# Reordering the head of a sparse-attention and mixer kernel: queries on ScalarE's queue, keys in two halves, and a new hand order

## The chip, the cores and the metric

The kernel runs on one core of one Trainium2 chip. The core has TensorE (PE) for matmuls, which writes its products to eight PSUM banks; VectorE (DVE), ScalarE (ACT) and GpSimd (POOL) for the rest; and 16 DMA engines, fed from queues that SyncE (SP), ScalarE and GpSimd issue to. All times are device microseconds. A kernel's time is the median over its runs. Beside the timed runs there is one profiled execution; its span, from its first to its last recorded work, is what the views of the profile divide up.

## The reference

Two steps are chained. The first is attention with a block-sparse mask over batch 4, 8 heads, 768 positions and head dimension 64. Positions fall into 24 blocks of 32. A query block sees its neighbours, the first and the last block, and three sampled blocks; the first and last query blocks see all.

```python
scores = scale * np.matmul(q, k.transpose(0, 1, 3, 2))
...
scores = np.where(mask, scores, -1000000000.0)
scores = scores - np.max(scores, axis=-1, keepdims=True)
attn = np.exp(scores)
attn = attn / (np.sum(attn, axis=-1, keepdims=True) + 1e-09)
return np.matmul(attn, v).astype(np.float32)
```

The second is a mixer on the attention's result x (4 x 768 x 512): a low-rank mixing over positions, then a channel network of width 2048.

```python
xt = x.transpose(0, 2, 1)
h = xt @ U @ V
u = x + h.transpose(0, 2, 1)
ch = np.maximum(u @ w_ch1, 0.0) @ w_ch2
return (u + ch).astype(np.float32)
```

Inputs and output are 32-bit floats; the kernel multiplies in 16 bits.

## The kernel before

**Tiles.** The 8 heads of a batch make 4 pairs, so there are 16 pairs (`NPAIR`). Per head, the 768 keys are 6 chunks of 128. A score product (`score`, L690) puts one key chunk against all 768 queries: two matmuls of 384 columns (L697) into two PSUM banks, followed by one exponential on ScalarE (L706). `two_scores` (L711) does two chunks at once in three banks: four matmuls (L716), one exponential over 1536 columns (L724). The exponentials of a chunk are the weights of six small matmuls with the values (`value_product`, L400), which sum over the chunks and give the numerator and, through a column of ones in `vts`, the denominator.

**The mask.** For the four pairs of batch 0 the mask is part of the product: beneath the 64 rows of a head's queries in `qres` stand 24 rows with a one-hot of the query's block, and beneath its keys in `kres` 24 rows with the bias (0 or -240) of that block for every key. For later batches the mask is a 0/1 tile (`mask`), made during the first pairs by `mask_part` (L654) from a copy of the bias rows (`kmask`) and multiplied on VectorE after the exponential (L756).

**The head of the kernel** is written out in order (L239 to L326). The sampled blocks, the first head's queries, keys and a constant `small` are loaded. `small` holds three things: the fixed mask, the block numbers, and a 128 x 128 identity in 16 bits (`id16`). VectorE computes the bias from the sampled blocks (L289 to L296). Loads are cast to 16 bits (`first_cast`, L208), turned by matmuls against the identity (`first_turn`, L214; three per half of the positions), and evicted to `qres[0]` and `kres[0]` (`first_row`, L281). `mask_half` (L270) multiplies the bias with the one-hot, and `mask_row` (L278) evicts it to the mask rows of one head for half of the keys. `keep_warm` (L262) issues matmuls on constants whose result nobody reads. The second head of the pair is cast on GpSimd and turned later (`last_turn`, L334, the word `Z`). The second buffers `qres[1]` and `kres[1]` and `kmask` are filled by `second_set` (L191): one-hots from memory, mask rows copied from the first set by DMA.

**The order.** On TensorE, VectorE, ScalarE and SP the program order is the order of work (`manual_schedule`); on GpSimd the same sequence arises. After the head, the order is the string `PLAN` (L432 to L457), of one word per step. A capital letter issues TensorE work, with the PSUM bank as digit: S and B are one and two score chunks, A one chunk's value product, Z and R turn queries or keys, K makes a part of the mask, M, X, Y, D and E mix over positions, P, C and U are products with `w_ch1` (L587), W and L with `w_ch2` (L611, L636), Q and H are scores of later batches (L741), V the values of a whole head there. A small letter issues what the oldest product of its kind still lacks on another engine: e an exponential, t, z, y, v, k, d, m and g evictions or sums on VectorE, p the multiplication by the mask, a or b a relu on ScalarE or VectorE, f and l the final sum and its store.

A product may not be written to a bank before the reader of its earlier content is done. `psm` (L107) hands out banks 2, 5 and 7 in turn, `psc2` (L100) banks 3 and 0; the two mask products lie in banks 6 and 2, the turned queries in banks 4 and 0, the turned keys in 5 and 7.

**Loads.** `load_qk` (L143) and `load_v` (L156) load a pair and cast it on GpSimd; `loads(i)` (L763) issues those of pair i + 2, the first when pair 0 begins. `w_ch1` is loaded on GpSimd's queue behind pair 3's loads, `w_ch2` by `hold` (L775) when pair 4 begins.

Of the kernel before, what the change touches and what calls it, by code (L numbers as in the profile page):

```python
# [19 lines left out]
P = 128  # L20
# [3 lines left out]
def kernel(  # L24
# [43 lines left out]
    small_np = np.zeros((P, NB + 1 + P // 2), np.float32)  # L68
    small_np[:NB, :NB] = (ms_np - 1.0) * -MASK_BIAS
    small_np[:NB, NB] = ii  # L70
    small_np[:, NB + 1 :] = np.eye(P, dtype=np.float16).view(np.float32)

    small_dr = nc.inline_tensor(small_np, name="small_const")
    ohT_dr = nc.inline_tensor(ohT_np, name="one_hot_const")
# [36 lines left out]
    small = consts.tile([P, NB + 1 + P // 2], FP32)  # L111
    ms = small[0:NB, 0:NB]
    iota = small[0:NB, NB : NB + 1]
    id16 = small[:, NB + 1 :].bitcast(FP16)
# [54 lines left out]
    def first_load(h, n, queue):  # L169

        src, nm = ((q, "qld"), (k, "kld"))[n]
        if h == 0:
            lds[nm] = ldpool.tile([P, 2, T, D], FP32, tag="ld" + nm, name=nm)
            sts[0, nm] = stpool.tile([P, T, 2, D], FP16, tag="st" + nm, name="st" + nm)
        if h == 1:
            nc.gpsimd.memset(lds[nm][0:1, h, 0, 0:1], 0.0)
        queue.dma_start(
            out=lds[nm][:, h], in_=src[0, h].rearrange("(p t) d -> p t d", t=T)
        )

# [10 lines left out]
    def second_set():  # L191
        for h in range(2):
            one_hot(1, h)
# [14 lines left out]
    def first_cast(h, n, copy):  # L208
        nm = ("qld", "kld")[n]
        copy(out=sts[0, nm][:, :, h], in_=lds[nm][:, h])  # L210
# [3 lines left out]
    def first_turn(n, c):  # L214

        if n == 1:
            pt = psm([P, HS], FP32)
        elif c == 0:
            pt = pw[:, 1, 0:HS]
        else:  # L220
            pt = psc2()[:, 0, 0:HS]
        first_out[n, c] = pt
        for j in range(3):
            nc.tensor.matmul(  # L224
                pt[0:D, j * P : (j + 1) * P],
                sts[0, ("qld", "kld")[n]][:, 3 * c + j, 0],
                id16,
                start=(j == 0), stop=(j == 2), skip_group_check=True,
            )

    with tc.manual_schedule(
# [13 lines left out]
        first_load(0, 0, nc.sync)  # L245
        nc.scalar.dma_start(out=small, in_=small_dr.ap())
        first_load(0, 1, nc.scalar)
        for h in (1, 0):
            nc.vector.memset(qres[0][(slice(D, P), slice(0, D))[h], h, :], 0.0)
            one_hot(0, h)  # L250
        nc.vector.memset(bias, 0.0)
# [26 lines left out]
        def mask_row(h, c, copy):  # L278
            copy(out=kres[0][mrows[h], h, c * HS : (c + 1) * HS], in_=pks[c][mrows[h]])

        def first_row(n, c, copy):  # L281
            copy(
                out=(qres, kres)[n][0][drows[0], 0, c * HS : (c + 1) * HS],
                in_=first_out[n, c][0:D],
            )

        neq = consts.tile([P, NB, 3], FP32)
# [14 lines left out]
        for n in range(2):  # L302
            first_cast(0, n, nc.vector.tensor_copy)
        for c in range(2):
            first_turn(0, c)
            first_row(0, c, nc.scalar.copy)
        mask_half(0)
        mask_row(0, 0, nc.vector.tensor_copy)
        first_turn(1, 0)
        first_row(1, 0, nc.scalar.copy)  # L310
        first_turn(1, 1)
        mask_half(1)
        keep_warm(2, 256)
        first_row(1, 1, nc.vector.tensor_copy)
        mask_row(0, 1, nc.vector.tensor_copy)
        mask_row(1, 0, nc.vector.tensor_copy)
        mask_row(1, 1, nc.vector.tensor_copy)
# [3 lines left out]
        nc.vector.memset(Ut, 0.0)  # L321
        load_v(0)
        load_qk(1)
        second_set()
        load_v(1)
        load_mix()  # L326


# [105 lines left out]
    S0 S3 e e S5 B0 e Z7 e S3 z Z6 e z B0 A7 A e R6 S3 t A R5 e A B0 t A K6 e A S3 k v A5 A e K6  # L434
    k B0 A A e K7 A K6 k S3 k A K7 e v B0 k S3 e M6 e A5 A m R7 A t B0 K6 R3 e k A A t S6 A e v
    S0 D2 S3 e d A7 A e A S0 K6 A e S3 k K2 A e S5 k A e v S3 R2 e S5 t S0 e M7 e S3 m D2 e B5 d
    A0 D1 e A A d A S3 D2 A e d K1 S5 k R7 e S3 t A S1 e v A5 A e A S3 S6 e K2 A e A k A S3 v B0
    e K7 M6 e k S3 m X5 K7 e A6 Y k A B0 y X7 Y e S3 y E5 A e A g A R7 S0 t A e v S4 S2 e A7 A e
    R1 E6 A t A g A A Q v e e M6 X7 m Y P6 y p H U7 e p H b C e p H b U7 e p H b U6 e p E1 a g p
    V7 Q v e e V6 U7 v p U0 a P1 b C p P6 a C E7 Q a g U6 e e U7 b P6 b p U0 C a U7 p a Q b X6 Y  # L440
    e e P7 y C P6 b C p U0 b a p V7 Q v e e V6 W7 v p U0 W a p Q U6 e e W b U6 p W b p Q f W6 e
    e W p U2 U0 a p a V7 Q v W e e p V7 U2 v W a p Q f W7 e e W p U6 W a p Q U6 e e W b U6 p f a
    p V0 U1 v a V7 U6 v Q a M6 e e W7 m W p D6 U0 d U1 p a D2 D3 a U6 d d D0 U5 a d D6 U1 a d W
    a W Q f D6 W7 e e d W p D0 D6 W d d p W Q f W6 e e W p W W p Q f e e V7 U6 v p a V0 U2 v p
    U7 a U6 a Q b U7 e e U6 b U7 b p U2 a U6 p a U7 a Q b U6 e e U7 b U6 b p U2 a p a V7 Q v e e
    V6 U7 v p U0 b U1 a W6 p a Q W e e W p W U7 f p Q a U6 e e W7 b W p U1 p a V6 Q v W e e p V6
    U2 v W a p Q f W6 e e W p U7 W b p Q U7 e e W b U7 p f U2 a p a V0 v V7 W6 v Q M7 e e W m U7
    p D0 U1 a d U2 p a D7 D3 a U0 d d U1 a D5 D0 a U2 d d U7 a W a W Q f D7 W6 e e d W p D1 D7 W
# [452 lines left out]
```

## Time and profile before

| what | value |
|---|---|
| median of 7 runs | 284.09 us (283.49 to 286.18) |
| profiled execution | 284.99 us |
| its span | 283.1 us |
| PE busy, share of span | 275.5 us, 97% |
| DVE busy | 194.3 us, 69% |
| ACT busy | 178.2 us, 63% |
| POOL busy | 74.1 us, 26% |
| first score on PE | 8.13 us |
| first exponential on ACT | 9.01 us |
| first `Q` on PE | 45.04 us |
| end of the last matmul in the chain | 276.9 us |

A busy PE is one that has a matmul in flight; their ends are modelled and overlap, so 97% is not 97% of its peak. Between 13.5 and 45 us three engines are nearly full (PE 31.1 of 31.5 us, ACT 29.9, DVE 28.1); between 48 and 226 us PE alone is (178.0 of 178.0, ACT 126.8, DVE 140.8). The granted clock (PEclk) reads full speed in every slice. In the lists below a line of the chain gives start, length and what it was; a line of a timeline gives start, length, engine, source line, operation, output and input with their shapes, how many, and in brackets the idle time before and what ended it.

### The profile page before, as it was taken

Reading aid. Unit: us, or ns where it says so; the run is one execution under the profiler, and the core shown is the slowest. Engines: PE = TensorE matmul, PEld = TensorE weight load, DVE = VectorE, ACT = ScalarE, POOL = GpSimd, SP = SyncE. Lnnn points to the kernel's source line nnn. Section 1 sums busy time; section 2 is a strip of 40 time slices with the busy share of each in tenths; the row PEclk is TensorE's granted clock in tenths of the full one; section 3 lists DMA queues with packets and bytes.
Section 4 is the critical chain, followed back from the end, with each engine's and each line's share of the span. In section 5 each row is a group of like instructions: output and inputs, shape, how many; then the busy total and the mean of one; then the engine's idle time right before and its main releaser. Section 6 shows DMA issues by size and latency. Waiting matters only on the chain.

```text
span 283.1 us, 6704 instructions
## 1 busy us (share of the span) xinstructions
PE 275.5 (97%) x2768; PEld 160.9 (57%) x2768; DVE 194.3 (69%) x347; ACT 178.2 (63%) x206; POOL 74.1 (26%) x164
## 2 busy tenths in 40 slices
PE   7899999999999999999999999999999999999993
PEld 3577775656464654656465654656546645555552
DVE  4599988998867898878677888777577871003411
ACT  3799998897687647687868555697876303551100
POOL 5367204926536050073443050070000000000000
PEclk9999999999999999999999999999999999999999
DMA  6699997999672564556260744641010062002021
GB/s 169 196 287 300 196 197 179 251 205 242 206 220 80 131 188 130 138 144 204 67 197 37 218 131 102 179 120 23 27 47 31 15 132 88 0 0 76 0 93 57
DMA packets 49118, 37.53 MB, mean 133 GB/s; under 512 B 30464, under 2 KB 45600, under 8 KB 49088
## 3 DMA queue, kind: packets, MB, share of 16 engines
q1 hardware_dynamic: 45968, 32.61, 41.9%
q0 software_dynamic: 2688, 4.19, 8.8%
q8 instruction: 21, 0.34, 0.5%
q10 hardware_dynamic: 432, 0.31, 0.4%
q14 instruction: 9, 0.07, 0.1%
HBM read 27.67 MB, written 6.29 MB: 120 GB/s over the span
## 4 chain that ended last, share of the span: by engine, by line
PE 91%; DVE 3%; DMA 2%; ACT 2%; issue 0%; SPq 0%; DVEq 0%; ACTq 0%
PE ps L587 30%; PE ps L611 29%; PE ps L400 12%; PE ps L741 10%; PE ps L697 3%; PE ps L529 2%; PE ps L716 2%; DMA qld<-in_q_dram 1%; ACT est L724 1%; ACT est L706 1%; PE ps L656 1%; DMA out_dram<-of 1%; DVE qres L686 1%; PE ps L636 1%; PE ps L670 1%; PE ps L224 1%
## 5 line engine op out<-in xcount | busy, mean ns | idle before, releaser
L750 ACT ACTIVATE est<-ps 128x1536 f16<-128x1536 f32 x72 | 100.4, 1451 | 38.6 <-PE ps L741 38.6
L587 PE MATMUL ps<-uT,w1t 128*128 128x384 f16 x512 | 94.3, 326 | 0.0
L611 PE MATMUL ps<-w2t,tT 128*128 128x512 f16 x368 | 87.1, 379 | 0.0
L756 DVE TENSOR_TENSOR est<-est,mask 128x1536 f16<-128x1536 f16 x72 | 69.6, 972 | 15.1 <-ACT est L750 14.9
L599 ACT ACTIVATE tT<-ps 128x384 f16<-128x384 f32 x90 | 43.1, 496 | 43.4 <-PE ps L587 42.2
L587 PEld LDWEIGHTS <-w1t 128*128 128x128 f16 x512 | 47.6, 98 | 36.3 <-issue 5.8
L611 PEld LDWEIGHTS <-tT 128*128 128x128 f16 x368 | 34.4, 98 | 39.6 <-issue 3.8
L400 PEld LDWEIGHTS <-est 128*128 128x128 f16 x1152 | 40.8, 97 | 7.0 <-issue 1.9
L400 PE MATMUL ps<-vt,est 128*128 128x65 f16 x1152 | 43.4, 193 | 0.0
L140 POOL CAST stqld<-qld 128x192 f16<-128x192 f32 x40 | 15.3, 423 | 85.5 <-DMA qld<-in_q_dram 59.9
L619 DVE TENSOR_TENSOR of<-xf,ps 128x512 f32<-128x512 f32 x23 | 15.7, 684 | 27.8 <-PE ps L611 25.8
L601 DVE TENSOR_SCALAR tT<-ps 128x384 f16<-128x384 f32 x38 | 21.1, 556 | 18.7 <-PE ps L587 18.1
L741 PE MATMUL ps<-qpl,kpl 64*128 64x512 f16 (+1 forms) x288 | 31.3, 325 | 0.0
L706 ACT ACTIVATE est<-ps 128x768 f16<-128x768 f32 x30 | 22.5, 815 | 1.5 <-PE ps L697 1.5
L741 PEld LDWEIGHTS <-kpl 64*128 64x128 f16 x288 | 11.8, 94 | 15.9 <-issue 10.4
L140 POOL CAST stkld<-kld 128x192 f16<-128x192 f32 x40 | 19.5, 528 | 1.3 <-DMA kld<-in_k_dram 1.3
L477 DVE TENSOR_TENSOR xh<-ps,rcp 128x384 f16<-128x384 f32 x32 | 17.8, 558 | 1.1
L477 DVE TENSOR_TENSOR xf<-ps,rcp 128x384 f32<-128x384 f32 x32 | 17.5, 548 | 0.0
L541 DVE TENSOR_TENSOR xh<-xh,ps 128x384 f16<-128x384 f16 x28 | 15.4, 551 | 1.7 <-PE ps L529 1.6
L542 DVE TENSOR_TENSOR xf<-xf,ps 128x384 f32<-128x384 f32 x28 | 15.4, 550 | 0.0
L140 POOL CAST vt<-vld 128x192 f16<-128x192 f32 x40 | 15.1, 416 | 0.5 <-DMA vld<-in_v_dram 0.5
L697 PE MATMUL ps<-qres,kres 128*128 128x384 f16 x60 | 14.7, 343 | 0.3
(83 smaller groups left out, 151.8 us busy)
## 6 DMA issues: line engine op xcount, KB each, us to landing
vld<-in_v_dram SPq DMA_DIRECT2D x16, 384.0 KB, 4.7
out_dram<-of SPq DMA_DIRECT2D x23, 256.0 KB, 2.0
qld<-in_q_dram SPq DMA_DIRECT2D x15, 384.0 KB, 5.1
kld<-in_k_dram SPq DMA_DIRECT2D x15, 384.0 KB, 4.9
w1t<-in_moe_w_ch_dram POOLq DMA_DIRECT2D x4, 512.0 KB, 8.2
w2t<-in_moe_w_ch_dram POOLq DMA_DIRECT2D x4, 512.0 KB, 7.9
qld<-in_q_dram SPq DMA_DIRECT2D x2, 192.0 KB
uT<-xh SPq DMA_TRANSPOSE x14, 2.8
```

Of the source, the lines that this page charges most:

```text
L140: last = nc.gpsimd.tensor_copy(out=dst[:, h, ts], in_=ld[:, h, ts])
L400: nc.tensor.matmul(pav[:, sc, :], est[:, n, sc * P : (sc + 1) * P], vts[b % 2][:, 2 * hp + h, g, 0 : D + 1], start=(g == 0 and sc == 0), s ...
L477: nc.vector.tensor_tensor(out=dst, in0=pav[:, :, 0:D], in1=rcp[:, :, None].broadcast_to([P, T, D]), op=ALU.mult,)
L587: nc.tensor.matmul(pt, w1t[:, cc, jj * P : (jj + 1) * P], bts[b].uT[cc][:, c * HS : (c + 1) * HS], start=(cc == 0), stop=(cc == NCC - 1), ...
L599: nc.scalar.activation(out=dst, in_=pt, func=AF.Relu)
L601: nc.vector.tensor_scalar_max(out=dst, in0=pt, scalar1=0.0)
L611: nc.tensor.matmul(po, tts[b, c, jj][:, s * P : (s + 1) * P], w2t[:, jj, :], start=(jj == 0), stop=(jj == NJJ - 1),)
L697: nc.tensor.matmul(ps[:, c], kT[:, h, g * P : (g + 1) * P], qT[:, h, c * HS : (c + 1) * HS], start=True, stop=True,)
L706: lambda: nc.scalar.activation(out=dst, in_=ps, func=AF.Exp, scale=0.125),
L741: nc.tensor.matmul(units[h][:, u * S + lo : u * S + hi], kT[drows[h], g * P : (g + 1) * P], qT[drows[h], lo:hi], start=True, stop=True, sk ...
L750: nc.scalar.activation(out=both[h], in_=units[h].rearrange("p (g n) -> p g n", g=2), func=AF.Exp, scale=0.125,)
L756: lambda: nc.vector.tensor_mul(out=both[h], in0=both[h], in1=mask[:, 2 * j : 2 * j + 2, :]),
```

## The change

The identity gets a constant of its own (`eye_dr`), so `small` shrinks to 24 rows of 25 numbers. The first load on ScalarE's queue is now the first head's queries, and the identity follows; on SP's queue stand the sampled blocks, `small`, the first half of the first head's keys (three of the six position groups), the two one-hots of the first set, and the second half of the keys. `first_load` and `first_cast` take a range of position groups for this.

Queries and the first half of the keys are cast on ScalarE, the second half on VectorE. `first_turn` uses the transposing form, which writes 16-bit values to PSUM. `first_row` and `mask_row` take a range of columns: the evictions of key chunk 0 come first, and those of chunks 1 and 2 after. The head ends once the second half of the keys is cast and the mask rows of head 0 are complete. What is left, turning the second half, its eviction, the mask rows of head 1 and the clearing of `Ut`, is a new function `second_keys`; it is called after the first two words of the plan, and behind it `second_set`, `load_v(1)`, `load_mix` and `loads(0)`. The one-hots of the second set move out of `second_set` to the end of the head. The two `keep_warm` matmuls of 256 columns go.

The plan is another string. It begins with a B (key chunks 0 and 1) in place of an S. Up to the first `Q` it has 26 S and 11 B where there were 30 S and 9 B, and the same number of every other capital letter; the banks and the places of many words differ throughout. Over the whole plan 45 relus are on VectorE and 83 on ScalarE, where there were 38 and 90. The first `W` is the 308th word and was the 295th.

```diff
--- before.py
+++ after.py
@@ -65,12 +65,12 @@
     cols = np.arange(S)
     blk = ((cols % P) * T + cols // P) // BLK
     ohT_np = (blk[None, :] == ii[:, None]).astype(np.float16)
-    small_np = np.zeros((P, NB + 1 + P // 2), np.float32)
-    small_np[:NB, :NB] = (ms_np - 1.0) * -MASK_BIAS
-    small_np[:NB, NB] = ii
-    small_np[:, NB + 1 :] = np.eye(P, dtype=np.float16).view(np.float32)
+    small_np = np.concatenate(
+        [(ms_np - 1.0) * -MASK_BIAS, ii[:, None].astype(np.float32)], axis=1
+    )
 
     small_dr = nc.inline_tensor(small_np, name="small_const")
+    eye_dr = nc.inline_tensor(np.eye(P, dtype=np.float16), name="eye_const")
     ohT_dr = nc.inline_tensor(ohT_np, name="one_hot_const")
 
     consts = ctx.enter_context(tc.tile_pool(name="consts", bufs=1))
@@ -108,10 +108,10 @@
         ring["psm"] += 1
         return bank((7, 2, 5)[ring["psm"] % 3], shape, dtype)
 
-    small = consts.tile([P, NB + 1 + P // 2], FP32)
+    small = consts.tile([P, NB + 1], FP32)
     ms = small[0:NB, 0:NB]
-    iota = small[0:NB, NB : NB + 1]
-    id16 = small[:, NB + 1 :].bitcast(FP16)
+    iota = small[0:NB, NB:]
+    id16 = consts.tile([P, P], FP16)
     sb = consts.tile([P, NB, 3, 2], I32)
     vts = [consts.tile([P, H, T, DV], FP16, name=f"vt{i}") for i in range(2)]
     NEST = 16
@@ -166,17 +166,20 @@
     NPAIR = B * HP
     lds = {}
 
-    def first_load(h, n, queue):
+    def first_load(h, n, queue, ts=slice(0, T)):
 
         src, nm = ((q, "qld"), (k, "kld"))[n]
-        if h == 0:
+        if nm not in lds:
             lds[nm] = ldpool.tile([P, 2, T, D], FP32, tag="ld" + nm, name=nm)
             sts[0, nm] = stpool.tile([P, T, 2, D], FP16, tag="st" + nm, name="st" + nm)
         if h == 1:
             nc.gpsimd.memset(lds[nm][0:1, h, 0, 0:1], 0.0)
         queue.dma_start(
-            out=lds[nm][:, h], in_=src[0, h].rearrange("(p t) d -> p t d", t=T)
-        )
+            out=lds[nm][:, h, ts],
+            in_=src[0, h].rearrange("(p t) d -> p t d", t=T)[:, ts],
+        )
+
+    halves = (slice(0, T // 2), slice(T // 2, T))
 
     def one_hot(i, h):
         nc.sync.dma_start(out=qres[i][mrows[h], h, :], in_=ohT_dr.ap())
@@ -190,7 +193,6 @@
 
     def second_set():
         for h in range(2):
-            one_hot(1, h)
             nc.sync.dma_start(out=kres[1][mrows[h], h, :], in_=kres[0][mrows[h], h, :])
         nc.sync.dma_start(out=kmask[mrows[0], :], in_=kres[0][mrows[0], 0, :])
 
@@ -205,27 +207,24 @@
             out=Vt[0:R, :, :], in_=vld[0:R, :].rearrange("r (p t) -> r t p", t=T)
         )
 
-    def first_cast(h, n, copy):
+    def first_cast(h, n, copy, ts=slice(0, T)):
         nm = ("qld", "kld")[n]
-        copy(out=sts[0, nm][:, :, h], in_=lds[nm][:, h])
+        copy(out=sts[0, nm][:, ts, h], in_=lds[nm][:, h, ts])
 
     first_out = {}
 
     def first_turn(n, c):
 
         if n == 1:
-            pt = psm([P, HS], FP32)
-        elif c == 0:
-            pt = pw[:, 1, 0:HS]
+            pt = psm([P, HS], FP16)
         else:
-            pt = psc2()[:, 0, 0:HS]
+            pt = (psc2()[:, 0] if c else pw[:, 1]).bitcast(FP16)[:, 0:HS]
         first_out[n, c] = pt
         for j in range(3):
-            nc.tensor.matmul(
-                pt[0:D, j * P : (j + 1) * P],
-                sts[0, ("qld", "kld")[n]][:, 3 * c + j, 0],
-                id16,
-                start=(j == 0), stop=(j == 2), skip_group_check=True,
+            nc.tensor.transpose(
+                out=pt[0:D, j * P : (j + 1) * P],
+                in_=sts[0, ("qld", "kld")[n]][:, 3 * c + j, 0],
+                identity=id16,
             )
 
     with tc.manual_schedule(
@@ -242,12 +241,14 @@
             .rearrange("z r -> (z r)")[None, :]
             .broadcast_to([NB, NB * 6]),
         )
-        first_load(0, 0, nc.sync)
-        nc.scalar.dma_start(out=small, in_=small_dr.ap())
-        first_load(0, 1, nc.scalar)
+        first_load(0, 0, nc.scalar)
+        nc.sync.dma_start(out=small[0:NB], in_=small_dr.ap())
+        first_load(0, 1, nc.sync, halves[0])
+        nc.scalar.dma_start(out=id16, in_=eye_dr.ap())
         for h in (1, 0):
             nc.vector.memset(qres[0][(slice(D, P), slice(0, D))[h], h, :], 0.0)
             one_hot(0, h)
+        first_load(0, 1, nc.sync, halves[1])
         nc.vector.memset(bias, 0.0)
         for h in range(2):
             nc.vector.memset(kres[0][(slice(D, P), slice(0, D))[h], h, :], 0.0)
@@ -275,15 +276,19 @@
                 start=True, stop=True,
             )
 
-        def mask_row(h, c, copy):
-            copy(out=kres[0][mrows[h], h, c * HS : (c + 1) * HS], in_=pks[c][mrows[h]])
-
-        def first_row(n, c, copy):
+        def mask_row(h, c, copy, lo=0, hi=HS):
             copy(
-                out=(qres, kres)[n][0][drows[0], 0, c * HS : (c + 1) * HS],
-                in_=first_out[n, c][0:D],
-            )
-
+                out=kres[0][mrows[h], h, c * HS + lo : c * HS + hi],
+                in_=pks[c][mrows[h], lo:hi],
+            )
+
+        def first_row(n, c, copy, lo=0, hi=HS):
+            copy(
+                out=(qres, kres)[n][0][drows[0], 0, c * HS + lo : c * HS + hi],
+                in_=first_out[n, c][0:D, lo:hi],
+            )
+
+        first_cast(0, 0, nc.scalar.copy)
         neq = consts.tile([P, NB, 3], FP32)
         a01 = consts.tile([P, NB], FP32)
         nc.vector.tensor_tensor(
@@ -299,32 +304,35 @@
             op0=ALU.mult, op1=ALU.max,
         )
         keep_warm(8)
-        for n in range(2):
-            first_cast(0, n, nc.vector.tensor_copy)
+        first_cast(0, 1, nc.scalar.copy, halves[0])
         for c in range(2):
             first_turn(0, c)
-            first_row(0, c, nc.scalar.copy)
-        mask_half(0)
-        mask_row(0, 0, nc.vector.tensor_copy)
         first_turn(1, 0)
-        first_row(1, 0, nc.scalar.copy)
-        first_turn(1, 1)
-        mask_half(1)
-        keep_warm(2, 256)
-        first_row(1, 1, nc.vector.tensor_copy)
+        for c in range(2):
+            mask_half(c)
+        first_row(0, 0, nc.scalar.copy)
+        first_row(0, 1, nc.vector.tensor_copy)
+        mask_row(0, 0, nc.vector.tensor_copy, 0, P)
+        first_row(1, 0, nc.scalar.copy, 0, P)
+        first_row(1, 0, nc.vector.tensor_copy, P)
+        mask_row(0, 0, nc.vector.tensor_copy, P)
+        first_cast(0, 1, nc.vector.tensor_copy, halves[1])
         mask_row(0, 1, nc.vector.tensor_copy)
-        mask_row(1, 0, nc.vector.tensor_copy)
-        mask_row(1, 1, nc.vector.tensor_copy)
 
         for n in range(2):
             first_cast(1, n, nc.gpsimd.tensor_copy)
-        nc.vector.memset(Ut, 0.0)
         load_v(0)
         load_qk(1)
-        second_set()
-        load_v(1)
-        load_mix()
-
+        for h in range(2):
+            one_hot(1, h)
+
+
+    def second_keys():
+        first_turn(1, 1)
+        first_row(1, 1, nc.vector.tensor_copy)
+        for c in range(2):
+            mask_row(1, c, nc.vector.tensor_copy)
+        nc.vector.memset(Ut, 0.0)
 
     results = {}
 
@@ -431,29 +439,29 @@
 
 
     PLAN = """
-    S0 S3 e e S5 B0 e Z7 e S3 z Z6 e z B0 A7 A e R6 S3 t A R5 e A B0 t A K6 e A S3 k v A5 A e K6
-    k B0 A A e K7 A K6 k S3 k A K7 e v B0 k S3 e M6 e A5 A m R7 A t B0 K6 R3 e k A A t S6 A e v
-    S0 D2 S3 e d A7 A e A S0 K6 A e S3 k K2 A e S5 k A e v S3 R2 e S5 t S0 e M7 e S3 m D2 e B5 d
...
+    B3 e S6 B0 e Z5 e S3 z Z7 e z A6 B0 A A e A S4 R7 e t R3 B0 t K5 K7 e A k k S3 A A5 e v B0 A
+    A e K7 K6 k A A k S3 A B0 e v K7 e M6 k S3 m K5 e R7 k A6 B0 t D5 A e S3 d R7 e A A t D5 S1
+    d A A e S3 v A7 A e S1 R0 e S3 t A e S5 A A e A S3 v B0 e K6 M5 e k S3 m e B5 A2 D0 e A R1 d
...
     """
 
     class Pair:
@@ -790,7 +798,7 @@
         elif i == HP + 2:
             for c in range(1, 4):
                 nc.sync.dma_start(out=Vt[c * R : (c + 1) * R], in_=Vt[0:R])
-        for m in {0: (0,), 1: (1, 2), 3: (3,), 4: (4,)}.get(i, ()):
+        for m in {1: (1, 2), 3: (3,), 4: (4,)}.get(i, ()):
             loads(m)
         if i == HP:
             hold(kpl[1])
@@ -858,7 +866,13 @@
             mybir.EngineType.SP,
         }
     ):
-        for word in PLAN.split():
+        for x, word in enumerate(PLAN.split()):
+            if x == 2:
+                second_keys()
+                second_set()
+                load_v(1)
+                load_mix()
+                loads(0)
             kind = word[0]
             if kind.isupper():
                 fn, *args = next(steps[kind])
```

## Prediction

> **What bounds the kernel now.** I read the views in this order: the page's chain by engine, the slices, the chain in order of time, then the timeline of ScalarE and TensorE over the first 16 us.
>
> ```profile
> span 283.1 us, 6704 instructions
> ...
> PE   7899999999999999999999999999999999999993
> ...
> PE 91%; DVE 3%; DMA 2%; ACT 2%; issue 0%; SPq 0%; DVEq 0%; ACTq 0%
> ```
>
> TensorE ends the kernel: from 48 us to 277 us nearly every piece of the chain is a matmul. The order after the first `Q` holds as many products of each kind in both plans, so the change can act in two places only: the head (0 to 13.5 us) and the stage of the first four head pairs (13.5 to 45 us). The chain opens so:
>
> ```profile
> 1.25 3.62 DMA qld<-in_q_dram
> ...
> 5.31 0.85 PE ps L224 x6
> 6.16 0.43 PE ps L271
> 6.59 0.78 PE ps L224 x6
> 7.37 0.43 PE ps L271
> 7.80 0.54 PE ps L264 x2
> 8.34 0.65 PE ps L697 x2
> ```
>
> Queries land at 4.88; eight microseconds are gone before the first score. ScalarE's timeline carries on from there:
>
> ```profile
> 9.01 2.22 ACT L706 ACTIVATE est<-ps 128x768 f16<-128x768 f32 x3 [1.45 <-PE ps L697]
> 11.10 1.47 ACT L724 ACTIVATE est<-ps 128x1536 f16<-128x1536 f32 x1
> 12.43 0.85 ACT L706 ACTIVATE est<-ps 128x768 f16<-128x768 f32 x1
> 13.47 1.45 ACT L724 ACTIVATE est<-ps 128x1536 f16<-128x1536 f32 x1 [0.19 <-PE ps L716]
> 14.82 0.81 ACT L706 ACTIVATE est<-ps 128x768 f16<-128x768 f32 x1
> 15.85 1.45 ACT L724 ACTIVATE est<-ps 128x1536 f16<-128x1536 f32 x1 [0.22 <-PE ps L716]
> ```
>
> From 9.01 to 44.7 ScalarE's 39 exponentials run almost without a break; the next, of the first `Q`, waits 1.2 us for TensorE. So this stage lasts as long as ScalarE needs. Back to back, an S costs 0.725 us (ten in 7.25) and a B about 1.365 (one of 1.47 overlaps its neighbour by a tenth): 30 x 0.725 + 9 x 1.365 = 34.0. The rest of the 35.7 is pauses of 0.2 to 0.35 before six B (1.5 us by the waits): a B on banks 0 to 2 cannot start while the last B's exponential reads them, and one S is too short to cover a B's matmuls.
>
> **The stage of the four pairs.** The new order has 26 S and 11 B: 26 x 0.725 + 11 x 1.365 = 33.87, **0.15 us less**. B after S after B on the same banks occurs six times in each order, so the pauses stay at 1.5. Matmuls, evictions and value products are the same in number, and after the last exponential both have four value products before `Q`. From the B of head 1 (the one at 13.47) the first banks agree but for one S. The saving of the head should therefore reach 45 us whole. Take 13.47 as the mark: when does that B start in the new kernel?
>
> **The head, loads.** Queries go from SP at 1.25 to ScalarE's queue at 0.75; the 44.5 KB constant no longer stands ahead there. SP then issues samples (0.75), mask constants (1.25), half of the keys (about 1.67), two one-hots and the second half (about 2.9). What is passed: the first loads of head 1 still wait for GpSimd's clearing at 3.24, so nothing behind is later, and the two one-hots of the second set leave SP's queue where 0.53 us of issue stood between the copies. Landing of queries: above 0.75 + 1.9 = 2.65 (the small constant took 1.9), below 0.75 + 3.62 = 4.37. Of keys: between 1.67 + 1.9 = 3.57 and 1.67 + 3.62 = 5.29. The Trainium skill ("DMA: Bandwidth & Descriptors", Issuing engines are not separate DMA queues) speaks against the split: transfers of all queues share 16 engines, and another queue saves the issue time alone. By that rule queries gain 0.5 us, landing at 4.38. By the rows, samples, constant, queries and keys of the old head (442 KB) were in by 5.03, some 2.4 us of flow at about 165 KB/us and near 0.85 of completion; now 250 KB stand up to the end of the queries and 336 KB up to half of the keys. That gives about 4.0 and 4.55. I take these, nearer the rows. The rule's value would delay queries' cast by 0.4 but the keys' by less than 0.4, since half the bytes are dropped.
>
> **The head, instructions.** Casts move from VectorE (0.36 each) to ScalarE, where a 384-column copy takes 0.47 (row of L282) and a half about 0.3. ScalarE is free from 3.15 (table load). Queued behind the keys' cast is the first eviction of queries, not needed sooner. Queries cast 4.0 to 4.5, keys 4.57 to 4.88. TensorE finishes its warm-up by 4.3, turns queries 4.55 to 5.2 (six at 0.107), keys' first half to 5.5, and runs both mask halves to 6.15. Evictions of turned rows are now 16-bit: L344 moves 768 such columns in 0.56 where L282 moves 384 of 32 bits in 0.55, so a 384-column row costs about 0.36. VectorE: queries' second row 5.37 to 5.73, mask of one chunk 6.02 to 6.3. First score at **6.35** instead of 8.13. It is a B: its second half needs VectorE's two further pieces (0.29 + 0.42, pipelined to 6.9).
>
> From here the clock counts. The 512-column warm-up matmuls stand 0.43 apart and the scores of 384 columns from 8.13 to 9.73 stand 0.32 apart, though the granted clock reads 1.00; from 10.0 on the same shapes take half. So the old head ran at half speed to about 9.9.
>
> - Full speed from about 6.5: B ends 7.45, ScalarE starts **7.5** instead of 9.01. VectorE casts the second key half (7.1), mask (7.6), turned keys (7.95), mask of head 1 (8.45). Only then are banks 6 and 7 free for S6: **a wait that the old order did not have**; behind it on TensorE stand B0, Z5 and S3, and ScalarE waits for them. S6's exponential 9.0, B0's 9.8, S3's 11.17; the B of head 1 has its banks at 11.2 and ScalarE starts it at **12.1**. Gain 1.37.
> - Half speed up to 9.9 as before: B ends 7.8, S6 starts 9.05, ends 9.87, B0 10.5, and the mark comes at **12.9**. Gain 0.57.
> - Half speed beyond: B0 ends 11.15, S3 12.4, the mark at **14.5**. Loss 1.03.
>
> The two removed warm-up matmuls (L264, 0.54 in the chain) are inside these sums. The skill ("TensorE: Matmul & The Clock Gate", Part 1) says full clock comes after one busy window of some 3.4 us with a free-running start. This trace agrees in kind: going back 3.4 us from 9.9 gives a window with almost no idle TensorE, while the one before it held the idle 4.3 to 5.3. In the new head that hole shrinks to about 0.3, which favours the first line; the new wait before S6 (7.6 or 7.95 to about 9) is a hole of 1 us in the next window, which is what speaks for the third.
>
> **Sum for the likeliest.** 1.37 + 0.15 = 1.52. The profiled execution took 284.99 (its span 283.1 and 1.9 around it) and would become 283.5; the median of the runs shown is 284.09, so **282.5**. Moving `W`: the first `W` at 69.7 ran without a pause in the old order, so its later place is worth nothing; the cover is the `U` products before it. Seven relus move to VectorE (0.55 against 0.5), which is idle over 20% from 48 us on: nothing, and should one be late a `W` waits for at most that 0.55.
>
> **Rivals.**
> - *Clock rises only at 9.9* (0.57 + 0.15): 283.4. For: same window position. Against: fuller TensorE from 0.8 to 7.
> - *The mechanism does nothing*: loads at their upper ends (keys cast at 5.6, 0.7 later) and half speed, or a new pause in the four pairs (K5 and K7 stand earlier; the kmask copy should land near 13, they run near 14.3): 284.1.
> - *Slower*: the wait of S6 for VectorE's chain keeps TensorE at half speed to about 13.3; 1.03 - 0.15 = 0.9, so 285.0, and 285.7 with loads at their upper ends. It decides when full speed comes later than about 11.5.
> - *The order saves pauses too*, up to 1.2 of the 1.5: 281.3.
>
> **How the numbers follow.** Likeliest 0.45 (own range 281.8 to 283.2), late clock 0.23, nothing 0.09, slower 0.18, better order 0.05. Leaving 2 in 10 outside: 281.3 to 285.3. The bound of 0.5% (about what a measurement can tell from no change) is 1.42 us, 282.67 and 285.51. Faster: 0.6 of 0.45, all of the better order, a third of the late clock: 0.40. Slower: most of that rival and of what no view foresees in a reordered plan: 0.18. Same: 0.42.
>
> **What would show it.** The first exponential, of 1536 columns, near 7.5, one pause of 0.1 to 0.7 before the second; matmuls of 384 columns 0.16 apart from 6.5 or 7; the mark near 12.1; the first `Q` near 43.5 instead of 45.04; after that every piece shifted alike. Wrong would be: keys landing after 5.3, half speed past 10, TensorE waiting for VectorE over 1.2 us before S6, or new pauses of ScalarE between 13 and 44.

## The result, and the profile after

The changed kernel took 285.68 us in the median of 27 runs (283.53 to 287.02, and two runs near 295 that the comparison leaves out); the kernel before took 284.80 in the median of 64 runs beside them. The ratio (of the runs without those two; it is not the quotient of the two medians) is 1.0015, with a 95% interval of 0.9993 to 1.0037: no difference that can be told from chance. The forecast was 282.5 with a range up to 285.3.

The profiled execution took 283.73 and would by itself have looked like a success. From its page: the span, TensorE's slices, and the chain by engine.

```profile
span 282.0 us, 6701 instructions
...
PE   8789999999999999999999999999999999999994
...
PE 84%; ACT 3%; DVE 1%; DMA 1%; issue 0%; ACTq 0%; DVEq 0%
```

TensorE still ends the kernel. ScalarE's timeline of the same execution (start, length, line, operation, idle time before and its cause):

```profile
6.93 1.45 ACT L732 ACTIVATE est<-ps 128x1536 f16<-128x1536 f32 x1 [1.61 <-PE ps L724]
8.72 0.81 ACT L714 ACTIVATE est<-ps 128x768 f16<-128x768 f32 x1 [0.34 <-PE ps L705]
9.43 1.45 ACT L732 ACTIVATE est<-ps 128x1536 f16<-128x1536 f32 x1
10.76 0.82 ACT L714 ACTIVATE est<-ps 128x768 f16<-128x768 f32 x1
11.91 1.45 ACT L732 ACTIVATE est<-ps 128x1536 f16<-128x1536 f32 x1 [0.33 <-PE ps L724]
...
16.04 0.81 ACT L714 ACTIVATE est<-ps 128x768 f16<-128x768 f32 x1 [0.33 <-PE ps L705]
...
45.19 4.14 ACT L758 ACTIVATE est<-ps 128x1536 f16<-128x1536 f32 x3 [1.20 <-PE ps L749]
```

The first exponential starts at 6.93 where the first profile of the old kernel had 9.01, and the mark of the prediction, the B of head 1, at 11.91 where that had 13.47: 1.56 us earlier. At the first exponential of `Q` 0.70 is left (45.19); in the first profile of the old kernel it was

```profile
45.89 2.79 ACT L750 ACTIVATE est<-ps 128x1536 f16<-128x1536 f32 x2 [1.20 <-PE ps L741]
```

On TensorE of the changed kernel stand these lines, with their waits for VectorE:

```profile
4.29 0.52 PE L224 MATMUL ps<-id,stqld 128*64 128x128 f16 x6
...
5.71 0.48 PE L724 MATMUL ps<-qres,kres 128*128 128x512 f16 x2 [0.31 <-DVE kres L280]
...
8.20 0.48 PE L705 MATMUL ps<-qres,kres 128*128 128x384 f16 x2 [1.02 <-DVE kres L280]
...
11.05 0.82 PE L724 MATMUL ps<-qres,kres 128*128 128x512 f16 x4 [0.54 <-DVE kres L352]
...
15.52 0.48 PE L705 MATMUL ps<-qres,kres 128*128 128x384 f16 x2 [0.65 <-DVE kres L694]
```

Six turning matmuls in 0.52 (0.85 in the old profile) say that TensorE was at full speed from about 4.3 us. So these two profiles differ in their clock as well as in their kernel, and the times of both kernels lie in separate groups: the old one's near 283.5, 284.8 and 286.0, the changed one's near 283.7, 285.7 and 286.7.

### The profile page after: what moved, and what is told of

It reads as the page before. It is cut to its first block, busy times and chain, and to the rows that moved or that the text cites. A ratio compares the mean times of both kernels' runs of the same rounds, so it can differ in the third digit from the quotient of the medians.

```text
span 282.0 us, 6701 instructions
## 1 busy us (share of the span) xinstructions
PE 273.5 (97%) x2766; PEld 158.9 (56%) x2766; DVE 198.1 (70%) x356; ACT 175.9 (62%) x198; POOL 76.4 (27%) x164
## 4 chain that ended last, share of the span: by engine, by line
PE 84%; ACT 3%; DVE 1%; DMA 1%; issue 0%; ACTq 0%; DVEq 0%
PE ps L595 30%; PE ps L619 29%; PE ps L749 10%; PE ps L408 10%; ACT est L714 2%; PE ps L537 2%; ACT est L732 1%; PE ps L724 1%; DMA out_dram<-of 1%; PE ps L644 1%; PE ps L574 0%; PE ps L506 0%; PE ps L521 0%; PE ps L705 0%; DVE of L627 0%; PE ps L515 0%
## 5 line engine op out<-in xcount | busy, mean ns | idle before, releaser
L758 ACT ACTIVATE est<-ps 128x1536 f16<-128x1536 f32 x72 | 100.4, 1451 | 36.4 <-PE ps L749 36.4
L764 DVE TENSOR_TENSOR est<-est,mask 128x1536 f16<-128x1536 f16 x72 | 69.7, 973 | 14.5 <-ACT est L758 14.4
L607 ACT ACTIVATE tT<-ps 128x384 f16<-128x384 f32 x83 | 39.9, 497 | 46.3 <-PE ps L595 34.1
L140 POOL CAST stqld<-qld 128x192 f16<-128x192 f32 x40 | 18.4, 500 | 86.0 <-DMA qld<-in_q_dram 43.6
L609 DVE TENSOR_SCALAR tT<-ps 128x384 f16<-128x384 f32 x45 | 24.9, 555 | 21.7 <-PE ps L595 20.8
L714 ACT ACTIVATE est<-ps 128x768 f16<-128x768 f32 x26 | 20.0, 813 | 0.9 <-PE ps L705 0.9
L140 POOL CAST vt<-vld 128x192 f16<-128x192 f32 x40 | 18.0, 486 | 1.1 <-DMA vld<-in_v_dram 1.1
L732 ACT ACTIVATE est<-ps 128x1536 f16<-128x1536 f32 x11 | 16.0, 1454 | 3.1 <-PE ps L724 3.1
L140 POOL CAST stkld<-kld 128x192 f16<-128x192 f32 x40 | 16.7, 454 | 0.6 <-DMA kld<-in_k_dram 0.6
```

Source lines behind the costliest of these rows:

```text
L140: last = nc.gpsimd.tensor_copy(out=dst[:, h, ts], in_=ld[:, h, ts])
L607: nc.scalar.activation(out=dst, in_=pt, func=AF.Relu)
L609: nc.vector.tensor_scalar_max(out=dst, in0=pt, scalar1=0.0)
L714: lambda: nc.scalar.activation(out=dst, in_=ps, func=AF.Exp, scale=0.125),
L732: lambda: nc.scalar.activation(out=est[:, s : s + 2, :], in_=ps.rearrange("p (g n) -> p g n", g=2), func=AF.Exp, scale=0.125,),
L758: nc.scalar.activation(out=both[h], in_=units[h].rearrange("p (g n) -> p g n", g=2), func=AF.Exp, scale=0.125,)
```

## The experiments

There are two theories. **Order**: the head's saving is real in every execution and the new order of the four pairs gives it back. **Clock**: executions of one kernel differ more by when TensorE reaches, and whether it keeps, full speed than by the change; the comparison of two profiles compared two clocks. A rival to the second is **load**: the groups come from transfers that land late. The mean clock of a run is its granted clock over the whole span; one stretch of 3.4 us at half speed takes 0.006 off it; what else is missing to 1 (up to 0.004 in the profiles) lies in the last microseconds of the span.

| run | median us | ratio to before | 95% interval |
|---|---|---|---|
| e1 before again | 284.32 | 1.0000 | 0.9974 to 1.0025 |
| e2 new head, old order | 283.23 | 0.9951 | 0.9922 to 0.9981 |
| e3 old head, new order | 285.56 | 1.0036 | 1.0011 to 1.0062 |
| e4 new head, new order to the mark, then old | 284.80 | 0.9985 | 0.9954 to 1.0017 |
| e5 changed kernel, five more warm-up matmuls | 284.36 | 0.9983 | 0.9964 to 1.0003 |
| e6 before, ten warm-up matmuls for eight | 283.64 | 0.9976 | 0.9956 to 0.9996 |
| e7, e11 as e2, five more warm-up matmuls | 283.68, 283.18 | 0.9965, 0.9957 | 0.9940 to 0.9990, 0.9937 to 0.9977 |
| e8, e12 as e16, five more warm-up matmuls | 283.05, 283.27 | 0.9937, 0.9970 | 0.9915 to 0.9960, 0.9950 to 0.9991 |
| e9 before, four warm-up matmuls for eight | 285.83 | 1.0043 | 1.0022 to 1.0063 |
| e10 changed kernel again | 285.41 | 1.0019 | 0.9994 to 1.0045 |
| e16 new head, old order to the first `Q`, then new | 283.23 | 0.9962 | 0.9938 to 0.9986 |

### The kernel before, a second profile (e1)

No edit.

> The kernel before, unchanged, profiled once more. Clock theory (executions differ by the moment at which TensorE reaches full speed, which moves from run to run, and the profiled execution of the kernel before was a late one, 9.9 us): times fall in groups near 283.4, 284.8 and 286.0; if the profile is of a run near 283.4, its 384-column scores stand 0.16 us apart by 8 us and the second head's B starts near 12, not 13.47; if near 286, full speed comes after 10 us. Order theory (the head's saving is real in every run and the new order of the four pairs gives it back): the second head's B starts at 13.5 whatever the time of the run, and the groups differ somewhere behind 45 us.

The profile was of a run of 283.50. Its lines on TensorE and ScalarE:

```profile
5.29 0.52 PE L224 MATMUL ps<-small,stqld 128*64 128x128 f16 x6 [0.96 <-DVE stqld L210]
...
6.96 0.99 PE L697 MATMUL ps<-qres,kres 128*128 128x384 f16 x5
...
8.47 0.32 PE L697 MATMUL ps<-qres,kres 128*128 128x384 f16 x1 [0.52 <-DVE kres L279]
...
11.16 0.82 PE L716 MATMUL ps<-qres,kres 128*128 128x512 f16 x4 [0.72 <-DVE kres L344]
...
7.50 2.21 ACT L706 ACTIVATE est<-ps 128x768 f16<-128x768 f32 x3 [0.59 <-PE ps L697]
...
12.02 1.45 ACT L724 ACTIVATE est<-ps 128x1536 f16<-128x1536 f32 x1 [0.26 <-PE ps L716]
...
15.74 0.80 ACT L706 ACTIVATE est<-ps 128x768 f16<-128x768 f32 x1
...
44.43 4.13 ACT L750 ACTIVATE est<-ps 128x1536 f16<-128x1536 f32 x3 [1.20 <-PE ps L741]
```

The old kernel, nothing changed, has its mark at 12.02 when TensorE is at full speed from the first turning matmul. Against that the new head gains 0.11 us, not 1.56, and at `Q` the changed kernel is 0.76 behind. The whole difference between the two profiles of the old kernel, 1.45 at the mark, is still there at `Q` (1.46) and in the span (1.4).

### Head and order exchanged (e2, e3, e4)

e2 and e3 exchange the strings, here seen from e2 (the rest is as in the changed kernel; this string and those below are wrapped anew, and the lines that follow are left out):

```diff
-    B3 e S6 B0 e Z5 e S3 z Z7 e z A6 B0 A A e A S4 R7 e t R3 B0 t K5 K7 e A k k S3 A A5 e v B0 A
+    S0 S3 e e S5 B0 e Z7 e S3 z Z6 e z B0 A7 A e R6 S3 t A R5 e A B0 t A K6 e A S3 k v A5 A e K6
...
```

> The new head (loads, casts, evictions, second_keys after two words) with the old order string. Order theory: the head's saving reaches the first Q whole, and the kernel is about 0.9 us faster than the changed one, near 282.8 in its fast group. Clock theory: no more than 0.5 us between this, the changed kernel and the kernel before in like groups; the groups stay 2 us apart.

> The old head with the new order string. Order theory: the pauses of ScalarE between the second head's B and the last S are 0.9 us longer than with the old string, and the kernel is about 1 us slower than before, 284.4 in its fast group. Clock theory: within 0.5 us of the kernel before, group by group.

e4 joins the new string's first 12 words to the old string from its second B on:

```diff
-    B3 e S6 B0 e Z5 e S3 z Z7 e z A6 B0 A A e A S4 R7 e t R3 B0 t K5 K7 e A k k S3 A A5 e v B0 A
+    B3 e S6 B0 e Z5 e S3 z Z7 e z B0 A7 A e R6 S3 t A R5 e A B0 t A K6 e A S3 k v A5 A e K6
...
```

> The new head with the new string's first 12 words (to the second head's first B), and from there the old string. Order theory: first exponential near 6.9 and the second head's B near 11.9 as in the changed kernel, from there on 31.2 us to the end of the last S as in the old order, first Q near 43.5; 0.9 us faster than the changed kernel. Clock theory: as the changed kernel, half of its runs near 285.7 with a mean clock of 0.994.

e2 is faster than the changed kernel and than the old one (its interval ends at 0.9981, that of the changed kernel begins at 0.9993); e3 is slower than the old one. In the profile of e4, at full speed from 4 us as that of the changed kernel was, ScalarE shows:

```profile
6.86 1.45 ACT L737 ACTIVATE est<-ps 128x1536 f16<-128x1536 f32 x1 [1.66 <-PE ps L729]
...
11.85 1.45 ACT L737 ACTIVATE est<-ps 128x1536 f16<-128x1536 f32 x1 [0.34 <-PE ps L729]
...
44.25 4.13 ACT L763 ACTIVATE est<-ps 128x1536 f16<-128x1536 f32 x3 [1.20 <-PE ps L754]
```

From the mark to `Q`: 32.40 in e4, 33.28 in the changed kernel (11.91 to 45.19), 32.41 in e1; in e3, the old head with the new string, 33.70. The order between these words costs **0.9 us**, as the order theory had it. One of its pauses can be read off the changed kernel's lines: S3 at 15.52 waits 0.65 for the eviction of turned keys (L694). R3 turns these keys in bank 3, where that score has to go, and VectorE evicts them between 14.34 and 15.46; the old string had them in bank 5. The exponential of this S starts 4.13 behind the mark (16.04), the one in its place in e1 3.72 (15.74): 0.41 of the 0.9. Two more new pauses of ScalarE come close behind (0.28 and 0.19 before 19 us). What those owe to this one, and where the rest is lost, was not tried.

e4's median is no better than the old kernel's all the same. Seven of its 14 runs lie between 284.3 and 285.0 with a mean clock of 0.991 to 0.992 and three near 282.5; the order theory cannot tell these apart. Its profiled run (285.85) was of neither kind: there TensorE waited 1.2 for transposed keys and 1.8 for the second weight matrix, at 67 and 77 us. So late loads can cost an execution time; no group of runs was traced to them.

### The clock, taken and given (e5, e6, e9)

```diff
             mask_half(c)
+        keep_warm(1)
         first_row(0, 0, nc.scalar.copy)
...
         first_turn(1, 1)
+        keep_warm(4, to=1)
         first_row(1, 1, nc.vector.tensor_copy)
```

(`to` names the bank; the lines of `keep_warm` that take it are left out.)

> The changed kernel with five more warm-up matmuls whose result nobody reads: one behind the mask halves, four behind the turning of the second key half, where TensorE waits for VectorE before S6. Clock theory (in about half of its runs the changed kernel reaches full speed near 4 us and loses it again for one stretch of 3.4 us, because TensorE waits in the new head: mean clock 0.991 to 0.994, 285.3 to 286.3): the group with 0.994 is gone, most runs near 283.7, median 283.8. Load theory (the groups come from transfers that land late, the second weight matrix or the transposed keys): the groups stay as they are, median 285.5.

The group with 0.991 to 0.994 is gone: all 22 runs have 0.997 or more. But half of them (11) lie from 284.2 to 284.7 and five near 285.6, not near 283.7, and the ratio (0.9983, up to 1.0003) is not clear of no change. In the profile, of a run of 284.28, full speed came at 5.1 and the mark at 12.29. The added matmuls do not hold up the first score there: it starts at 6.09, and in a profile without them whose full speed came at 5.3 (e14, below) at 6.19. What is lost against 5.71 is the later clock.

```diff
-        keep_warm(8)
+        keep_warm(10)
```

> The kernel before with ten warm-up matmuls in place of eight, so that TensorE has work to about 5.1 us, when queries are cast. Clock theory: the runs near 286.0 (full speed late) become runs near 283.5 or 284.8; less than 1 in 6 above 285.5 where it was 1 in 3; median near 283.6. Load theory: a third of the runs stays near 286.

Twenty of 22 runs lie between 283.3 and 284.3, two above 286; of the 61 runs of the old kernel beside them 19 lay above 285.8 and 22 between 284.2 and 285.1. Two matmuls that nobody reads, in the hole in which TensorE waits for queries, move the old kernel's median by 1.2 us (ratio 0.9976). No load was touched for that.

```diff
-        keep_warm(8)
+        keep_warm(4)
```

> The kernel before with four warm-up matmuls in place of eight: TensorE idles from about 2.5 to 5.3 us. Clock theory: no run reaches full speed near 4 us; the group at 283.4 is gone, all runs lie near 284.8 or 286, full speed in the profile comes at 8.5 us or later, and the second head's B starts at 13 or later. Load theory: the groups stay in the proportions that the kernel before has.

No run is under 284.6, and 12 of 17 lie from 285.5 to 286.3. The profile is of one at 286.12:

```profile
9.96 1.49 PE L716 MATMUL ps<-qres,kres 128*128 128x512 f16 x4
...
11.88 0.84 PE L697 MATMUL ps<-qres,kres 128*128 128x384 f16 x2
...
14.64 1.45 ACT L724 ACTIVATE est<-ps 128x1536 f16<-128x1536 f32 x1 [1.01 <-PE ps L716]
```

Four matmuls of a B take 1.49 at 9.96 and 0.81 in a profile at full speed; half speed lasts past 12 us and the mark comes at 14.64. The old kernel's three groups are thus: full speed near 4 us (mark 12.0, 283.5), near 10 (13.5, 284.9), past 12 (14.6, 286.1). The last was seen in e9 only, whose times and mean clock (0.996) are those of the old kernel's own group; the old kernel itself was not caught there.

### The changed kernel, four more profiles (e10, e13, e14, e15)

No edit.

> The changed kernel, profiled once more. If its time is near 285.7: clock theory expects the clock's records to show half speed for 3.4 us somewhere between 5 and 14 us and the second head's B at 13 or later; load theory expects a wait for a transfer behind 45 us. If it is near 283.7, the marks of the first profile again (6.9, 11.9, 45.2).

> The changed kernel, profiled a third time. If its time lies near 285.7 with a mean clock of 0.994: the clock theory expects the records to show full speed first, then half speed for 3.4 us inside the head (between 5 and 14 us), then full speed; and the second head's B at 13.5 or later. The load theory expects the lost time behind 45 us.

> The changed kernel, profiled a fourth time, with the same expectation: a run near 285.7 shows the clock lost inside the head; a run near 286.6 shows it reached late, near 12 us; a run near 283.7 shows it reached near 4 us and kept.

> The changed kernel, profiled a fifth time, with the same expectation as the fourth.

e10 (284.39) had full speed from about 6 us and its mark at 12.56. e14 took 285.88 with a mean clock of 0.994, as in the group that the clock theory is about. Its stretches (length; busy time of PE, PEld, DVE, ACT and POOL; granted clock; DMA share; GB/s):

```profile
8.00:9.00 1.00, 0.32 (x2) 0.16 (x2) 1.00 (x3) 0.86 (x1) 0.00 (x0) 0.87 1.00 329
9.00:10.00 1.00, 1.00 (x5) 0.50 (x4) 0.47 (x2) 0.51 (x1) 0.71 (x1) 0.50 0.89 329
10.00:11.00 1.00, 1.00 (x8) 0.66 (x7) 0.00 (x0) 0.53 (x2) 0.77 (x2) 0.50 0.45 143
11.00:12.00 1.00, 1.00 (x8) 0.66 (x7) 0.52 (x1) 1.00 (x1) 0.84 (x2) 0.50 0.62 63
12.00:13.00 1.00, 0.66 (x13) 0.53 (x10) 0.46 (x2) 0.93 (x2) 0.15 (x1) 0.93 0.55 189
```

Granted 0.87, three times 0.50 and 0.93: 0.26 + 3.0 + 0.14 = 3.4 us at half speed, beginning near 8.7, at the end of the wait that the new head brought. Its lines:

```profile
7.30 0.35 PE L224 MATMUL ps<-id,stkld 128*64 128x128 f16 x3
8.68 0.78 PE L705 MATMUL ps<-qres,kres 128*128 128x384 f16 x2 [1.02 <-DVE kres L280]
9.25 1.49 PE L724 MATMUL ps<-qres,kres 128*128 128x512 f16 x4
...
14.06 1.45 ACT L732 ACTIVATE est<-ps 128x1536 f16<-128x1536 f32 x1 [1.13 <-PE ps L724]
```

TensorE waits 1.02 for VectorE's mask rows before S6, B0 then takes 1.49, the mark comes at 14.06. The first profile had the same wait (1.02) and kept its clock, so the wait alone does not decide. In e13 and e15 (286.73, 286.70) full speed came only past 13 us and the mark at 14.79 and 14.80. The marks of the other three:

```profile
12.56 1.45 ACT L732 ACTIVATE est<-ps 128x1536 f16<-128x1536 f32 x1 [0.34 <-PE ps L724]
...
14.79 1.45 ACT L732 ACTIVATE est<-ps 128x1536 f16<-128x1536 f32 x1 [1.32 <-PE ps L724]
...
14.80 1.45 ACT L732 ACTIVATE est<-ps 128x1536 f16<-128x1536 f32 x1 [1.32 <-PE ps L724]
```

In all five profiles of the changed kernel the mark to `Q` takes the same 33.3 us, and in none of them does TensorE wait for a transfer behind 45 us, as the load theory had it: the clock's part is over by the mark. The trace's clock records begin with the change to full speed, so its moment can be set beside the mark. Both go together in both kernels:

| full speed from, us | mark, old kernel | mark, changed kernel |
|---|---|---|
| 4.2 (e1), 4.3, kept | 12.02 (e1) | 11.91 (first profile) |
| 6.0 | | 12.56 (e10) |
| 9.9 | 13.47 (first profile) | |
| 5.3, lost from 8.7 to 12.1 | | 14.06 (e14) |
| 12.6 (e9), 13.2 (e13), 13.6 (e15) | 14.64 (e9, four warm-up matmuls) | 14.79 (e13), 14.80 (e15) |

### A version that beats both (e7, e8, e11, e12, e16)

e7 and e11 are e2 with e5's added matmuls (four of them to bank 5). e16 takes the new head, the old string up to the first `Q` and the new one from there; e8 and e12 are e16 with the added matmuls. Here is the seam of e16, seen from the changed kernel (what stands ahead of these words is exchanged too):

```diff
-    E0 A e A g A K6 A k A Q v e e M6 X7 m Y P6 y p H U7 e p H b C e p H b U7 e p H b U6 e p E2 a g p V7 Q v e
+    S4 S2 e A7 A e R1 E6 A t A g A A Q v e e M6 X7 m Y P6 y p H U7 e p H b C e p H b U7 e p H b U6 e p E2 a g p V7 Q v e
...
```

> The new head with the old order and the same five warm-up matmuls. Clock theory: one group near 282.6 to 283.2, nothing with a mean clock under 0.995, median 282.8, 0.7% under the kernel before. Load theory: still some runs near 285.3, where the second weight matrix is late.

> As the run before it, but from the first Q on with the new order, whose first W comes later. If a late second weight matrix costs time in some runs of the old order: fewer runs above 284.5 than in the run before it, and median up to 0.5 us lower. If the new order behind the first Q is worth nothing: the same times within 0.3 us. If it costs something by itself: slower by what it costs, in every group.

> The new head with the old order and five more warm-up matmuls, profiled once more. Half of its runs lay near 284.5 with a mean clock of 1.0. If the profile is of such a run: load theory expects TensorE to wait for the second weight matrix or for transposed keys between 60 and 80 us, by 1.5 us or more; clock theory expects half speed past 8 us.

> The version with the new head, the old order up to the first Q and the new one from there, with five more warm-up matmuls, timed once more: 0.992 to 0.996 of the kernel before, nearly all runs under 283.5, since the later first W leaves the second weight matrix time to land and the filled head keeps the clock.

> The new head, the old order up to the first Q and the new order from there, without added warm-up matmuls. Clock theory: best runs near 282.5, but a group with a mean clock of 0.992 to 0.994 near 284.7, which the filled version does not have; median between 283.2 and 284.5. If the added matmuls are only a cost: all runs 0.3 us below the filled version.

All of these are 0.3 to 0.6% faster than the old kernel, and their intervals overlap: the new head with the old order of the four pairs is what they share. Part of their gain lies where nobody expected it. e2's profiled run took 282.72, 0.78 less than e1, and both were at full speed from 4.1 or 4.2:

```profile
11.65 1.45 ACT L737 ACTIVATE est<-ps 128x1536 f16<-128x1536 f32 x1 [0.34 <-PE ps L729]
...
44.30 4.13 ACT L763 ACTIVATE est<-ps 128x1536 f16<-128x1536 f32 x3 [1.20 <-PE ps L754]
```

With the old order the new head gains 0.37 at the mark, of which 0.13 is left at `Q` (0.35 in e16) and 0.12 at the last matmul. The other 0.6 lies behind the last matmul. These are the last matmuls of the first profiles, old (span 283.1) and changed (span 282.0):

```profile
276.69 1.95 PE L636 MATMUL ps<-w2t,tT 128*128 128x128 f16 x32
...
276.17 1.95 PE L644 MATMUL ps<-w2t,tT 128*128 128x128 f16 x32
```

From their end the span goes on for 4.4 or 4.5 us in all five profiles with the old head and for 3.8 in all thirteen with the new one, whatever the order and the clock. The last packets of the final stores land 2.6 us behind that end in all eighteen, so the difference lies in what the engines still wait for behind the stores. Why the new head shortens these was not tried.

The new order behind `Q` gives nothing in the times (e16 and e2 have the same median), and on TensorE it costs 0.17: from `Q` to the end of the last matmul e16 takes 232.92, e2 232.76 and e1 232.75. The later first `W` is thus worth nothing in nearly every run. The added matmuls trade one group for another. Without them 6 of e16's 22 runs have a mean clock of 0.991 to 0.992 and lie near 284.8; with them none of e12's has, but 6 lie near 284.8 with 1.0. e11's profile (284.70) shows why:

```profile
8.42 1.86 PE L265 MATMUL ps<-const-bfloat16-1.0 128*128 128x512 bf16 x4
10.10 0.50 PE L712 MATMUL ps<-qres,kres 128*128 128x384 f16 x2
```

Where the clock is not up yet the four added matmuls take 1.86 instead of 1.04 (e7) and stand before the score. Late loads, which were expected there, show no wait in this profile. The group of e12 was not profiled.

## Why the prediction was wrong

**Step by step the head went as predicted**, and somewhat earlier. In the first profile queries landed by 3.4 (4.0 forecast), half of the keys by 4.0 (4.55): for queries the rows came nearer than the skill's rule that another queue saves its issue time alone (4.38). It brought little, as TensorE's warm-up lasts to 4.3. The first score stood at 5.71 (6.35), the first exponential at 6.93 (7.5), the new wait before S6 was 1.02 with a pause of 0.34 on ScalarE (0.1 to 0.7), the mark at 11.91 (12.1). The match at the mark is in part luck: full speed came at 4.3, not at the assumed 6.5, and where it came at 6.0 (e10) the mark was 12.56. The line for a clock that comes up late said 14.5; 14.06 and 14.8 were measured.

**The step that failed is the subtraction.** The sum took 13.47 - 12.1 = 1.37 as the gain of the head. 13.47 belongs to an execution at half speed to 10 us, 12.1 to one at full speed from 6.5. The text saw that the old head "ran at half speed to about 9.9" and took that for a property of the kernel; e1 shows that it belongs to one execution, as the same kernel has 12.02. Clock for clock the head gains 0.11 where full speed comes early (11.91 against 12.02) and nothing that shows where it comes late (14.8 against 14.64 in e9). The first score starts over a microsecond earlier (5.71 against 6.96 in e1) and gains next to nothing at the mark: in both kernels the mark stands behind VectorE's chain of evictions, up to the keys of head 1 (the wait of 0.72 for L344 in e1, of 0.54 for L352 in the changed kernel), and in the new head S6, and with it the Z behind it, stands behind that chain as well (1.02 for L280, where S5 waits 0.52 for L279 in e1).

**"Should reach 45 us whole" failed too.** The pauses were counted by the pattern B, S, B on the same banks, which is the same in both orders; a bank shared by a turning step and a score was not looked for. The term "pauses stay at 1.5" was too small by 0.9 (33.28 against 32.41 from the mark to `Q`). The saving of fewer exponentials (0.15) is too small to be seen beside it.

**The rival on the other side was right and given too little.** That the wait before S6 keeps TensorE at half speed was given 0.18. Nine of the changed kernel's 25 runs up to 287.02 have the mean clock of such a loss (0.991 to 0.994; 0.994 in e14), and five more lie at 286.58 to 287.02, where e13 and e15 reached full speed later still. What that rival lacked is that the old kernel pays for its own hole (the idle time before its first turning matmul), in about as many runs. The sum that the runs support, from e1 to the first profile of the changed kernel: 0.11 gained in the head, 0.87 lost up to `Q`, 0.18 lost from there to the last matmul, 0.63 gained behind the last matmul and 0.08 outside the span, which makes the 0.23 between 283.50 and 283.73; and a clock that is late or lost about as often as before. The gain behind the last matmul stood in no forecast: without it the changed kernel would have been slower by about 0.2% more.

For the clock the prediction leaned on the Trainium skill ("TensorE: Matmul & The Clock Gate", Part 1), which says that the window in which activity is judged runs freely and does not restart with the kernel. It used that rule to choose among clocks for the new kernel, and not for the old one, whose two profiles reached full speed at 9.9 and 4.2. The 3.4 us lost in e14 agree with the window's length on that page.

## What to carry to other kernels

Before a saving at the start of a kernel is subtracted, profile several executions of the unchanged kernel: if its times form groups, one profile shows one of them, and the start times in it are not the kernel's. A hole in TensorE's first microseconds has a price of its own beyond the wait, and it is paid some microseconds later (here up to 12 or 13); filling the hole with two matmuls that nobody reads (e6, 0.9976) was worth a good part of what the new head brings with the old order (e2 and e16, 0.9951 and 0.9962; the intervals overlap). When an order is written out by hand, check each bank's last reader against the next step that writes it, since a turning step in a score's bank (R3) stops the scores until VectorE has evicted it (0.65 here). And compare two kernels piece by piece, to the very end of the span: 0.6 us of this change lies behind the last matmul.

## What the runs showed of the hardware

Full speed arrives at a moment that differs between executions of one program: at 4.2 or 9.9 us in two profiles of the old kernel, at 4.3, 5.3, 6.0, 13.2 and 13.6 in those of the changed one. The groups of times it makes are up to 3 us apart (1%).

It can also be lost soon after it came, with TensorE partly at work in the stretch before. In e14 the records read 3.41 us at full speed, 3.41 at half, then full; in e3 the same, from 3.7 us on. The long stretches at full speed behind that are whole multiples of this length in every profile (from 269.65 to 279.89 us, 79 to 82 times 3.413). In these traces the clock thus changes on a raster of 3.413 us that starts at another point in each execution.

How full of work a stretch must be to raise or keep the clock, and of what work, stays open. e1 kept full speed across an idle time of 0.96 us before its first turning matmul; e3, with 1.21 us there, lost it (0.85 granted on average over its first 10 us). In e9 TensorE shows no pause between the raster points at 5.8 and 9.2 us, and full speed came only at 12.6: pauses are not all that counts. Whether turning matmuls count as full work was not tried.

The granted clock reads 1.00 from the start of the span although the spacing of matmuls shows half speed (warm-up matmuls of 512 columns stand 0.43 us apart): the record starts with the first change. Ahead of that the spacing is what can be trusted.
